# An attention and mixture-of-experts kernel: 128 tokens of the leading expert as a slot of their own, in plain fp32, and that expert first in the ring

## The chip, the cores and the metric

One core of one Trainium2 chip runs the whole kernel in one launch. The metric is device time in microseconds (us). PE is TensorE (PEld its weight loads), DVE is VectorE, ACT is ScalarE, POOL is GpSimd, SP is SyncE, from which most DMAs are issued.

## The reference

Attention with a memory term for 4 batches of 576 tokens, 8 heads of 64; its output is x (2304 tokens of 512). A gate picks one of 8 experts for each token. The expert is a two-layer network whose result is scaled by two gate factors.

```python
logits = x @ w_gate                       # 2304 x 8
e_idx = np.argmax(logits, axis=1)
probs = softmax(logits)
gate_w = probs[np.arange(N), e_idx]
eom = 1.0 / (1.0 + np.exp(-(x @ w_output_gate)))
for e in range(8):
    mask = e_idx == e
    h = np.maximum(x[mask] @ w1[e], 0.0)  # 512 -> 1024
    ye = h @ w2[e]                        # 1024 -> 512
    out[mask] = gate_w[mask, None] * eom[mask, e, None] * ye
```

On the inputs used, routing gives the eight experts 2, 465, 120, 834, 36, 680, 12 and 155 tokens. In the first two batches it gives them 0, 62, 120, 441, 2, 527, 0 and 0.

## The kernel before

**Attention.** The work is cut into jobs (scores `SS`, maxima `M`, exponentials `E`, transposes `T`, their copies `V`, values `P`, memory products `ME`, and so on), and the string `ORDER` is the order in which they are issued to the engines, written out by hand: each engine runs its own jobs in that order. Batches 0 to 2 are routed inside attention (`RT`, `RK`, `CA`, `CJ`, `CB`, `SEL`), the last one behind it. `rank` counts with small matmuls the tokens that go to an expert before each token; `cntb` carries the counts from batch to batch. The finished x goes to `xs` in DRAM, the gate factors to `gd`.

**Between attention and loop.** The last batch is routed (`route`, `rank`, `tail_rank`). From the counts come the first slot of each expert (`slots1`, `slots2`) and, through `place` (40 small matmuls into `pp`, L999) and `rows` (L1004), the token numbers of each slot. A slot is 128 tokens of one expert; tokens beyond its number are empty. `gather` (L1069) fetches a slot's x by row number; `gather_gate` (L1065) its gate factors. While PE waits, `warm` (L163) issues matmuls of ones whose results nobody reads.

**The loop.** There are 25 slots at most (NSLOT). 23 of them (NMAIN) always run; the two others stand behind a branch on the number of slots used. A product of fp32 numbers is made of three products in fp32r: x and the weights are split into a high part (a cast) and a low part (the rest), and high·high, low·high and high·low are added. `gemm1` gives h (24 matmuls of 512 columns, L1121) and its relu (ACT L1134); `stage_h` transposes h (`hp`, 8 transposes, L1144), copies it and splits it (`hh` on ACT, `hl` on POOL L1149); `gemm2` gives y (24 matmuls into `py`, L1121). `stage_x` transposes x (`px`, 4 transposes) and splits it (`xh`, `xl`). On PE the order is gemm1(s + 1), px(s + 2), the first half of gemm2(s), hp(s + 1), the second half of gemm2(s). `scatter` (L1172) writes the rows.

**Weights.** Each expert has eight raw chunks of 512 KB (four of w1, four of w2), fetched on SP's queue into a ring of five buffers. DVE casts each into `whi` (L961) and subtracts into `wlo` (L964), in turn. `whi` and `wlo` hold two experts, by the parity of the expert's turn. `sem_w` counts the chunks that are ready, and gemm waits on it. `load_expert` is the refill for turns 2 to 7: the first four chunks wait on `sem_1` until gemm1 of the last slot of the expert two turns before is done (`lim`), the last four on `sem_2` until its gemm2 is. Experts run in the order of their numbers.

```python
def load_expert(e):
    for c in range(8):
        fetch(e, c)
        if c == 0:
            lim = V.value_load(limi[0:1, e - 2:e - 1], min_val=1, max_val=NMAIN)
        if c % 4 == 0:
            V.wait_ge(sem_2 if c else sem_1, lim)
        high(e, c, V)
        low(e, c)
        ready()
```

Of the kernel before, what the change touches and what calls it, by code (L numbers as in the profile page):

```python
# [10 lines left out]
F32 = mybir.dt.float32  # L11
# [14 lines left out]
E = 8  # L26
# [8 lines left out]
NSLOT = 25  # L35
NMAIN = 23
# [46 lines left out]
N12_2 V11_3_0:ACT Tgate41 N22_2 E11_2_0 SS12_3 W2 T11_2_1 V11_2_1:ACT T11_2_0 SEL1_3 SS12_4 E12_1_0 PV2_1 T12_0 load_v14 V11_2_0:ACT E12_1_1 V12_0:ACT
M12_3_1 M12_3_0 F215 P11_256_0 G2_2 SEL1_4 M12_4_0 Y2_1 E12_3_1 E12_3_0 SS13_1 P11_256_1 M12_4_1 SEL1_2 T12_1 M13_0_0 T12_3_1 M13_1_0 O11_256:ACT
M13_0_1 V12_1:ACT M13_1_1 E12_4 XD2_1 PV2_4 PV2_3 R14 Y2_4 E13_1_1 T12_3_0 E13_0_1 SS12_2 SS13_3 XD2_4 OUT2_1 OUT2_4 V12_3_1:ACT V12_3_0:DVE M12_2_1
G2_4 E13_1_0 GA1 E13_0_0 T12_4 Y2_3 CA1 V12_4_0:ACT E12_2_1 F014 LT2_0 M12_2_0 LT2_1 T13_0 F012 SEL1_1 XD2_3 V12_4_1:DVE T13_1 LC2_0:DVE LC2_1:ACT
# [4 lines left out]
V13_4_0:ACT E14_3_1 N23_4 V13_4_1:ACT E14_1_0 SS15_4 M14_3_0 SEL0_0 T14_0 ME3_2 SS14_4 V14_0:DVE M15_4_0 N13_2 N23_2 M15_4_1 T14_1 M14_4_0 E14_3_0
M14_4_1 T14_3_0 ME3_0 SS15_1 V14_1:ACT E15_4 V14_3_0:ACT N13_0 N23_0 SS14_2 M15_0_0 T14_3_1 M15_1_1 E14_4 OUT2_0 G3_4 M15_1_0 M15_0_1 OUT2_2
V14_3_1:ACT Tgate61 fetch2 E15_0_0 P13_256_0 T14_4 CJ1 P13_256_1 P14_0_0 V14_4_0:DVE TS15_0 E15_1_1 G3_1 W3_0 CB1 V14_4_1:ACT TS15_1 O14_0:DVE
O13_256:ACT E15_0_1 TS14_1 T15_4 PLl4_0 M14_2_1 PLl1_0 V15_4_0:ACT fetch3 YLl4_0 TL4_0 E14_2_1 YLl1_0 T15_0 XLl4_0 PLl0_0 YLl0_0 V15_4_1:ACT V15_0:ACT
# [32 lines left out]
def attn_moe(ctx: ExitStack, tc: tile.TileContext, qk, vd, mz, mt, rz, beta, wgo, w1, w2, out):  # L127
# [72 lines left out]
    def rank(b):  # L200
# [7 lines left out]
        if last:  # L208
# [1102 lines left out]
```

## Time and profile before

| what | us |
|---|---|
| median of 3 runs (lowest, highest) | 515.14 (514.45, 515.40) |
| the profiled execution, its own time | 514.72 |
| its span, first to last instruction | 512.6 |
| PE busy in the span | 496.0 |
| DVE, ACT, POOL busy | 333.1, 282.0, 307.0 |
| mean granted TensorE clock | 0.994 of full |

Attention takes about the first 200 us, the loop with its start the rest. A busy PE counts every instruction in flight, dummies too. Full clock is 2.4 GHz, a granted clock of 0.50 is 1.2 GHz. An fp32 product that is not a transpose leaves two PE records, an fp32r product or a transpose one.

### The profile page before, as it was taken

How to read it: one execution, taken by the hardware profiler on the slowest of the kernel's cores; microseconds unless marked ns; L12 is line 12 of the kernel's file. 1: busy time of each engine (PE TensorE's matmuls, PEld its weight loads, DVE VectorE, ACT ScalarE, POOL GpSimd, SP SyncE). 2: the span in 40 equal slices, each digit the busy share in tenths (PEclk: the TensorE clock that was granted, in tenths of full speed). 3: DMA queues.
4: the chain of work that ended last, by engine and by line, in shares of the span. 5: the costliest groups of instructions: out<-in, count | busy, mean ns of one | idle time of the engine just before them, and what ended most of it. 6: DMA issues, size and time to landing. Idle time of an engine off the chain costs nothing.

```text
span 512.6 us, 10898 instructions
## 1 busy us (share of the span) xinstructions
PE 496.0 (97%) x3408; PEld 395.5 (77%) x3408; DVE 333.1 (65%) x819; ACT 282.0 (55%) x650; POOL 307.0 (60%) x287
## 2 busy tenths in 40 slices
PE   7999999999999998979999999999999999999995
PEld 4787778787877875557888888888888888888885
DVE  4988989889789879679898389300074892026510
ACT  5989888988787764263333344434434333333441
POOL 8756565665447327636777767565557675556333
PEclk9999999999999999989999999999999999999998
DMA  7442345241413602486687467511153674115000
GB/s 250 158 172 84 130 136 184 102 165 47 141 46 99 192 3 84 126 336 206 190 239 208 131 192 243 166 63 43 41 177 112 193 221 139 63 41 165 8 3 29
DMA packets 27233, 68.25 MB, mean 133 GB/s; under 512 B 4308, under 2 KB 4840, under 8 KB 27178
## 3 DMA queue, kind: packets, MB, share of 16 engines
q1 hardware_dynamic: 22602, 56.63, 34.6%
q0 software_dynamic: 4432, 10.77, 6.3%
q8 instruction: 33, 0.54, 0.4%
q14 instruction: 22, 0.18, 0.1%
q10 hardware_dynamic: 144, 0.13, 0.1%
HBM read 58.06 MB, written 10.76 MB: 134 GB/s over the span
## 4 chain that ended last, share of the span: by engine, by line
PE 87%; DVE 4%; DMA 3%; issue 2%; POOL 1%; ACT 1%; POOLq 0%; SPq 0%; DVEq 0%; ACTq 0%
PE h L1121 23%; PE py L1121 22%; PE po L624 9%; PE pt L589 8%; PE s L514 7%; PE me L676 4%; PE hp L1144 4%; PE sd L501 3%; PE pt L558 2%; PE px L1090 2%; DMA raw<-in_w 2%; DVE wlo L964 1%; PE pv L739 1%; PE pl L844 1%; DVE whi L961 1%
## 5 line engine op out<-in xcount | busy, mean ns | idle before, releaser
L961 DVE CAST whi<-raw 128x1024 fp32r<-128x1024 f32 x56 | 57.4, 1025 | 115.3 <-issue 82.4
L1149 POOL TENSOR_TENSOR hl<-hT,hh 128x512 fp32r<-128x512 f32 x46 | 68.3, 1505 | 73.6 <-ACT hh L1148 73.6
L964 DVE TENSOR_TENSOR wlo<-raw,whi 128x1024 fp32r<-128x1024 f32 x63 | 97.1, 1541 | 7.0 <-ACT whi L961 4.7
L1121 PE MATMUL py<-whi,hh 128*128 (+1 forms) x192 | 77.9, 406 | 0.7 <-DVEq L967 0.7
L1121 PE MATMUL h<-whi,xh 128*128 (+1 forms) x184 | 73.6, 400 | 1.8 <-ACT xh L1095 1.7
L1121 PE MATMUL h<-whi,xl 128*128 (+1 forms) x184 | 73.7, 401 | 1.6 <-POOL xl L1098 1.6
L1121 PE MATMUL py<-wlo,hh 128*128 (+1 forms) x192 | 74.2, 386 | 0.0
L1121 PE MATMUL py<-whi,hl 128*128 (+1 forms) x192 | 73.8, 384 | 0.0
L577 ACT ACTIVATE st<-st,nm 128x128 f32<-128x128 f32 (+3 forms) x128 | 71.6, 562 | 3.4 <-DVE nm L572 3.2
L1121 PE MATMUL h<-wlo,xh 128*128 (+1 forms) x184 | 73.2, 398 | 0.0
L572 DVE CUSTOM_DVE_ANT_0 st<-s,mask 128x128 f32<-128x128 f32 (+3 forms) x128 | 58.3, 483 | 9.9 <-PE s L514 5.4
L1134 ACT ACTIVATE h<-h 128x1024 f32<-128x1024 f32 x23 | 23.6, 1027 | 73.3 <-PE h L1121 73.3
L409 POOL TENSOR_TENSOR lo<-qk,hi 128x1216 fp32r<-128x1216 f32 x15 | 42.1, 2810 | 23.3 <-ACT hi L405 17.9
L1148 ACT CAST hh<-hp 128x512 fp32r<-128x512 f32 x46 | 27.6, 599 | 47.3 <-PE py L1121 47.3
L436 ACT COPY PT<-pt 128x512 f32<-128x512 f32 (+2 forms) x89 | 45.2, 523 | 15.1 <-PE pt L589 13.1
L1147 ACT COPY hT<-hp 128x512 f32<-128x512 f32 x46 | 27.2, 592 | 42.1 <-PE hp L1144 40.6
L624 PE MATMUL po<-PT,v 128*64 128x320 f32 (+4 forms) x480 | 48.9, 349 | 0.3 <-DVE gs L281 0.3
L589 PE MATMUL pt<-ident,st 128*128 128x128 f32 x320 | 47.5, 280 | 0.0
L1121 PEld LDWEIGHTS h<-whi,xh 128*128 128x128 f32 x184 | 34.9, 189 | 10.8 <-ACT xh L1095 2.2
L1121 PEld LDWEIGHTS h<-whi,xl 128*128 128x128 f32 x184 | 35.0, 190 | 10.3 <-POOL xl L1098 1.9
L624 PEld LDWEIGHTS po<-PT,v 128*64 128x64 f32 x480 | 29.7, 137 | 17.1 <-issue 2.9
L1121 PEld LDWEIGHTS py<-wlo,hh 128*128 128x128 f32 x192 | 36.1, 188 | 8.1
(204 smaller groups left out, 988.8 us busy)
## 6 DMA issues: line engine op xcount, KB each, us to landing
raw<-in_w SPq DMA_DIRECT2D x64, 512.0 KB
qk<-in_qk SPq DMA_DIRECT2D x15, 640.0 KB
v<-in_vd SPq DMA_DIRECT2D x16, 320.0 KB
xs<-xd SPq DMA_DIRECT2D x12, 256.0 KB
mz<-in_mz SPq DMA_DIRECT2D x4, 324.0 KB
mt<-in_mt SPq DMA_DIRECT2D x4, 256.0 KB
xs<-xa SPq DMA_DIRECT2D x4, 256.0 KB
xs<-xd SPq DMA_DIRECT2D x3, 128.0 KB
```

Source lines behind the costliest of these rows:

```text
L409: G.tensor_tensor(c["lo"][:, TQ:], c["raw"][:, TQ:], f32(c["hi"])[:, TQ:], op=ALU.subtract)
L436: (A.copy if e == "ACT" else V.tensor_copy)(dst(), src())
L514: T.matmul(c()["ss", q][j], l[r, lc], m[r, KC:KC + w], start=(a == 0), stop=(a == 2))
L572: V.tensor_tensor_reduce(st[:, :w], c()["ss", qt][j], mask[:, 512 - w:512], -SCALE, 3.0e38, ALU.add, ALU.min, negm()[:, i:i + 1])
L577: A.activation(st, st, AF.Exp, bias=c()["negm"][:, i:i + 1], scale=-1.0, accum_out=sums()[:, qt, 2 * p + j:2 * p + j + 1])
L589: T.transpose(pt[:, (m * k1 + i) * P:(m * k1 + i + 1) * P], st[:, i * P:(i + 1) * P], ident)
L624: T.matmul(po[64 * j:64 * j + 64, qs - q0:q1 - q0], vt[:, k, 64 * j:64 * j + 64], PT[:, j, k, qs:q1], start=(k == 0), stop=(k == kn - 1))
L961: join((A.copy if eng is A else eng.tensor_copy)(whi[:, e % 2, c, :], raws[e, c]))
L964: join(eng.tensor_tensor(wlo[:, e % 2, c, :], raws.pop((e, c)), f32(whi[:, e % 2, c, :]), op=ALU.subtract))
L1121: i = T.matmul(o[n % nh], l[:, z], m[:, n * 512 + part.start:n * 512 + part.stop], start=(c == 0 and k == 0 and n < nh), stop=(c == 3 and ...
L1148: A.copy(hh[:, z], hp[:, z])
L1149: G.tensor_tensor(hl[:, z], hT[:, z], f32(hh)[:, z], op=ALU.subtract)
```

## The change

Tokens are counted after batches 0 and 1, inside attention. The expert with the highest count there (the star) gives 128 of its tokens of these batches to a slot of its own, `e`. Its rows are found by ten small matmuls (`ZP`) and gathered; its x is transposed (`ZX`, `ZY`). The star's raw weights are fetched during attention (five chunks in place of four, at an address read from a register) and behind it (three). Its two layers are computed from the raw weights in plain fp32, 8 products of 512 columns each, spread over the stretch between attention and loop, where the `warm` matmuls are taken out.

The rest of the star's tokens come first in the ring, then the other experts in the order of their numbers: `order` holds that, and every fetch reads it. The ring has one slot less: NSLOT 24, NMAIN 22. The weights of turn 0 are split as before, but the chunks of w2 behind the star's products; turn 1 is split by DVE alone. A slot waits for all four chunks of a layer at once, except slot 0, which still waits chunk by chunk.

Smaller parts: tiles that outlive the routing stand in pools of their own; the attention outputs of odd batches stand where h32 and hT of the loop stand later; the gates of the last batch are computed behind the row numbers, beside the fp32 products; x of slot 0 is split as that of any other slot (`stage_x` in place of `first_x`).

```diff
-NSLOT = 25
-NMAIN = 23
+NSLOT = 24
+NMAIN = 22
...
 # in ORDER (new names only, with what stands around them)
+... Tpos21 CA1 CJ1 CB1 SS11_2 ... T11_4 ZC M11_2_1 E11_3_0 TS11_1 M11_2_0 Z1 Z2 Tpos31 load_v12 M12_0_0 Z3 Z4
+G2_1 V11_4_0:DVE Z5 P11_0_0 ... Tpos41 Z6 Z7 E12_0_0 Tgate21 M12_0_1 Z8 Z9 Z10 ... M12_1_1 ZN ME2_2
+... M14_3_0 SEL0_0 SEL1_0 ZK T14_0 ... T14_1 ZP M14_4_0 ZR ZG E14_3_0 ... PLl2_0 ZX YLl2_0 ZY XLl0_0 ...
+P15_512_0 fetch4 P15_0_0
...
+    def star_number():
+        V.tensor_scalar(which, ze["m"], -1.0, float(E), op0=ALU.mult, op1=ALU.add)
+        V.scalar_tensor_tensor(order[:, 1:], seven[:, 1:], which, seven[:, 1:], op0=ALU.is_ge, op1=ALU.add)
+        V.tensor_copy(order[:, 0:1], which)
...
+    def star_place():
+        ze["p"] = psm.tile([P, 1], F32, name="zp", tag="m")
+        for t in range(half_tiles):
+            T.matmul(ze["p"], selp.rearrange("p b t c -> p (b t) c")[:, t, :], stars[:, t:t + 1], start=(t == 0), stop=(t == half_tiles - 1))
...
+    def star_turn():
+        ze["px"] = pst.tile([P, 512], F32, name="pxe", tag="pt")
+        for c in range(4):
+            T.transpose(ze["px"][:, c * P:(c + 1) * P], ze["x"][:, c * P:(c + 1) * P], ident)
...
-    warm(6)
+    def star_gemm1(n, cs):
+        for c in cs:
+            T.matmul(he[:, n * 512:(n + 1) * 512], ze["x", c], raws[0, c][:, n * 512:(n + 1) * 512], start=(c == 0), stop=(c == 3))
...
+    def star_gemm2(ks):
...
+        for k in ks:
+            T.matmul(ze["py"], hTe[:, k * P:(k + 1) * P], raws[0, 4 + k // 2][:, k % 2 * 512:k % 2 * 512 + 512], start=(k == 0), stop=(k == 7))
+
+    star_gemm1(0, range(3))
     for f in route(B - 1):
         f()
     for c in range(2):
         high(0, c, A)
     rank(B - 1)
+    star_gemm1(0, range(3, 4))
+    star_relu(0)
+    star_gemm1(1, range(4))
+    star_h(0)
...
         rows(0)
         rows(1)
-        warm(10)
+        star_relu(1)
+        star_h(1)
...
-    warm(12)
     rx.close()
...
-                last = c0 + (c + 1 if s < 4 else 4)
                 if s == 0:
-                    T.wait_ge(sem_w, last + c0)
-                elif s < 4 or c == 0:
-                    T.wait_ge(sem_w, t["need", c0] + last)
+                    T.wait_ge(sem_w, c0 + c + 1)
+                elif c == 0:
+                    T.wait_ge(sem_w, t["need"] + (c0 + 4))
...
+    for c in (5, 6):
+        fetch_star(c, sx.tile([P, F], F32, name=f"star{c}", tag="raw"))
     gather(0)
+    low(0, 0)
+    ready()
+    fetch_star(7, raw_tile("star7"))
+    for f in fin["gates"][0]:
+        f()
+    for c in range(2, 4):
+        high(0, c, A)
+    gather_gate("e")
     gather(1)
...
+    for c in range(1, 4):
         low(0, c)
         ready()
...
+    star_gemm2(range(6))
+    stage_x(0)
+    for f in fin["gates"][1]:
+        f()
+    star_gemm2(range(6, 8))
+    finish_star()
     counts()
+    gather_gate(0)
+    gather(2)
+    gemm1(0, lambda: stage_x(1))
+    regs(1)
+    gather_gate(1)
+    gather_gate(2)
+    gather(3)
+    for c in range(4, 8):
+        split(0, c, V)
+    for c in range(8):
         fetch(1, c)
+        split(1, c, V)
```

## Rows read from the trace of the kernel before

**Rows 1.** The page, part 4: the chain that ended last, by engine
```profile
PE 87%; DVE 4%; DMA 3%; issue 2%; POOL 1%; ACT 1%; POOLq 0%; SPq 0%; DVEq 0%; ACTq 0%
```

**Rows 2.** Windows: stretch, PE, PEld, DVE, ACT, POOL busy (instructions), clock, DMA, GB/s
```profile
100.00:200.00 100.00, 99.32 (x1001) 78.80 (x998) 85.59 (x342) 75.72 (x213) 50.34 (x59) 1.00 0.31 102
```

**Rows 3.** Timeline, 190 to 225: start, us, engine, line, operation, out<-in, count [idle <-releaser]
```profile
198.27 1.35 PE L844 MATMUL pl<-rzt,oT 128*128 128x160 f32 x8
...
199.77 1.46 PE L163 MATMUL warm<-ones 128*128 128x512 bf16 x6
...
202.86 1.89 PE L163 MATMUL warm<-ones 128*128 128x512 bf16 x8
...
205.38 1.16 PE L999 MATMUL pp<-hit,selp 128*128 128x4 f16 x40 [0.64 <-DVE hit L996]
206.06 0.16 DVE L1004 TENSOR_SCALAR rowi<-pp 128x4 int32<-128x4 f32 x1 [0.32 <-PE pp L999]
...
212.93 0.50 PE L1121 MATMUL h<-whi,xh 128*128 128x512 f32 x1
...
220.41 0.58 ACT L1095 CAST xh<-px 128x512 fp32r<-128x512 f32 x1
...
221.56 1.47 POOL L1098 TENSOR_TENSOR xl<-x,xh 128x512 fp32r<-128x512 f32 x1 [3.39 <-ACT x L1097]
```

**Rows 4.** Chain in order of time, 200 to 300: start, us, engine, tile, line, count
```profile
207.94 3.79 DMA xr<-xs,rowi
...
215.89 7.88 DMA raw<-in_w
...
238.93 5.60 PE h L1121 x24
```

**Rows 5.** Chain in order of time, 340 to 420
```profile
357.15 0.44 PE px L1090 x4
357.59 2.81 PE py L1121 x12
360.39 0.87 PE hp L1144 x8
361.27 2.80 PE py L1121 x12
364.06 5.60 PE h L1121 x24
...
401.60 5.60 PE h L1121 x24
```

**Rows 6.** Timeline of DVE, 262 to 513: the refill of the weights
```profile
370.92 0.71 DVE L961 CAST whi<-raw 128x1024 fp32r<-128x1024 f32 x1 [45.30 <-issue]
...
391.47 1.53 DVE L961 CAST whi<-raw 128x1024 fp32r<-128x1024 f32 x1 [9.60 <-ACTq L1128]
...
402.67 1.60 DVE L961 CAST whi<-raw 128x1024 fp32r<-128x1024 f32 x1 [0.87 <-issue]
404.30 2.20 DVE L964 TENSOR_TENSOR wlo<-raw,whi 128x1024 fp32r<-128x1024 f32 x1
406.64 0.69 DVE L961 CAST whi<-raw 128x1024 fp32r<-128x1024 f32 x1
407.37 1.23 DVE L964 TENSOR_TENSOR wlo<-raw,whi 128x1024 fp32r<-128x1024 f32 x1
...
411.55 2.51 DVE L964 TENSOR_TENSOR wlo<-raw,whi 128x1024 fp32r<-128x1024 f32 x1
```

**Rows 7.** Timeline of POOL, 398 to 416
```profile
402.43 3.00 POOL L1149 TENSOR_TENSOR hl<-hT,hh 128x512 fp32r<-128x512 f32 x2 [3.81 <-ACT hh L1148]
...
411.67 1.30 POOL L1098 TENSOR_TENSOR xl<-x,xh 128x512 fp32r<-128x512 f32 x1
```

**Rows 8.** Windows of PE alone: stretch, PE busy (instructions), clock, DMA, GB/s
```profile
223.00:223.50 0.50, 0.41 (x1) 0.50 1.01 362
...
226.00:226.50 0.50, 0.50 (x4) 0.75 1.03 385
```

More of the change, by code (lines that the diff above doesn't have):

```diff
@@ L83 @@
[L83 to L86, printed above, removed]
@@ L91 @@
[L91 to L94, printed above, removed]
@@ L99 @@
-OL4 RX2 GO1 RK2 V15_2_0:ACT CA2 Tpos12 Tgate32 Tpos22 Tgate22 CJ2 T15_2_1 Tpos32 Tgate42 V15_2_1:ACT GA2 CB2 Tgate52 P15_384_0 O15_384:ACT P15_256_0
-Tpos42 Tgate62 TL0_1 TL3_0 XLl3_0 XLl0_1 PLl3_1 G3_3 SEL2_0 OL1 O15_256:ACT SEL2_3 SEL2_2 SEL2_4 G3_2 SEL2_1 PLl2_1 YLl3_1 YLl2_1 XLl3_1 XLl2_1 GP2
-GS2 OL0 OL2 OL3 GO2 TL2_1 TL3_1
+V10_4_0:ACT MW3 T11_0 M11_4_0 Tpos11 M11_3_0 load14 TS10_1 V10_4_1:ACT V11_0:ACT MC3 T11_1 M11_3_1 V11_1:ACT ME2_4 Tpos21 CA1 CJ1 CB1 SS11_2 M11_4_1
+E11_4 SS12_1 E11_3_1 N12_4 N22_4 T11_4 ZC M11_2_1 E11_3_0 TS11_1 M11_2_0 Z1 Z2 Tpos31 load_v12 M12_0_0 Z3 Z4 G2_1 V11_4_0:DVE Z5 P11_0_0 TS11_0
@@ L154, in attn_moe @@
     less = const.tile([P, E], BF16, name="less")
-    back = const.tile([P, E], F32, name="back")
+    back = const.tile([P, NEND], F32, name="back")
+    star = const.tile([P, E], F32, name="star")
+    rest8 = const.tile([P, E], F32, name="rest8")
+    order = const.tile([P, E], I32, name="order")
+    seven = const.tile([P, E], F32, name="seven")
+    later = const.tile([P, E], F32, name="later")
+    gone = const.tile([P, NEND], F32, name="gone")
+    which = const.tile([P, 1], F32, name="which")
+    stars = const.tile([P, NQ * 2], F16, name="stars")
+    begin = const.tile([P, E], F32, name="begin")
+    rowe = const.tile([P, 1], I32, name="rowe")
+    lg3 = const.tile([P, NQ, 16], F32, name="lg3")
+    gs3 = const.tile([P, P], F32, name="gs3")
+    dl3 = const.tile([P, NQ, E], F32, name="dl3")
+    og3 = [const.tile([P, NQ], F32, name=f"{n}3") for n in ("og", "gw")]
+    ze = {}
     ohe = const.tile([P, B * NQ, E + 1], F32, name="ohe")
@@ L925, in attn_moe, with star_total @@
         pair(g)
-    for c in range(4):
-        job(f"fetch{c}", "SP", 400, 60 + 2 * c, fetch, 0, c, after=[f"load{NG - 1}", "R15"] + ([f"fetch{c - 1}"] if c else []), takes=[("qa" if c < 2 else "hi", f"raw{c}")], size=512)
+    for c in range(5):
+        job(f"fetch{c}", "SP", 400, 60 + 2 * c, lambda c: fetch_star(c) and None, c)
+    half_tiles = 2 * NQ
+    jc = ohe[:, :half_tiles, E]
+    def star_total():
+        ze["n"] = psm.tile([P, E], F32, name="zn", tag="m")
+        T.matmul(ze["n"], ones, cntb, start=True, stop=True)
@@ L928, in attn_moe, with star_columns_of @@
+    def star_columns_of():
+        for c in range(4):
+            A.copy(ze["x", c], ze["px"][:, c * P:(c + 1) * P])
+    job("ZY", "ACT", 800, 0.0, star_columns_of)
     for b in range(B):
@@ L1180, in split @@
         ready()
+    for c in (5, 6):
+        fetch_star(c, sx.tile([P, F], F32, name=f"star{c}", tag="raw"))
     gather(0)
+    low(0, 0)
[6 more added lines that the diff above has]
+    gather_gate("e")
     gather(1)
-    gather(2)
-    for c in range(2):
+    for c in range(1, 4):
         low(0, c)
         ready()
-    low(0, 3, G)
-    for c in range(2):
-        fetch(1, c, sx, None if c else st[0]["x"][0:1, 0:1])
-    low(0, 2)
-    ready()
-    first_x()
-    for s in range(3):
-        gather_gate(s)
-    V.tensor_copy(top[0:1, 0:1], f32(wlo)[0:1, 0, 3, 0:1])
-    ready()
-    counts()
-    for c in (2, 3):
-        fetch(1, c)
-    for c in range(2):
-        split(1, c, A)
-    def second():
-        stage_x(1)
-        for c in (2, 3):
-            split(1, c, A)
-    gemm1(0, second)
-    regs(1)
-    gather(3)
-    for e in range(2):
-        for c in range(4, 8):
-            fetch(e, c)
-            split(e, c, V)
+    star_gemm2(range(6))
[4 more added lines that the diff above has]
+    finish_star()
+    counts()
+    gather_gate(0)
[8 more added lines that the diff above has]
+    for c in range(8):
+        fetch(1, c)
+        split(1, c, V)
     for s in range(NMAIN):
```

241 lines of the change are left out of this document (163 added, 78 removed).

## The prediction, made before the changed kernel ran

> **What bounds the kernel now.** I read the chain of waits by engine first [rows 1]: 87% of the span is TensorE (PE), so a change counts where it alters PE's queue or makes PE wait. Then the windows: in attention PE is busy 99.32 of 100 us, with VectorE (DVE) at 85.59 beside it [rows 2], so matmuls added there lengthen it one for one, while DVE work has some slack.
>
> Then the stretch between attention and loop [rows 3]. PE is never off for long there, but much of what it does is dummy work: the 8 `warm` matmuls after the rank take 1.89 us, and 36 are issued in all, at 0.24 us some 8.5 us. They hold nothing up: the slot positions (`pp`, 40 small matmuls) come at 205.38, when DVE delivers `hit`, and the row numbers at 206.06. The chain of that stretch [rows 4] shows the gather of the first tokens (3.79 us), and later 7.88 us of waiting for raw weights. Slot 0's first product is at 212.93 and slot 2's at 238.93. What PE computes between is 2 first products, 1 second product and their transposes.
>
> Last, the loop [rows 5]. One period is px 0.44, 12 py 2.81, hp 0.87, 12 py 2.80, 24 h 5.60: 12.52 us, without gap. A slot fewer is worth **12.52 us** if nothing else stalls. By these lengths the work from slot 0's first product to slot 2's is 5.60 + 0.44 + 5.60 + 0.87 + 0.44 + 2.81 + 0.87 + 2.80 = 19.43 us; it took 26.00. So the start loses 6.6 us, since slots 0 and 1 belong to two experts whose weights are still arriving.
>
> **What the new order of experts does.** The reference's routing on its inputs gives 2, 465, 120, 834, 36, 680, 12 and 155 tokens: slots 1, 4, 1, 7, 1, 6, 1, 2, in all 23. Expert 5 leads the first half with 527. With 128 of its tokens taken out and itself in front, the ring is 5 (slots 0 to 4), 0 (slot 5), 1 (6 to 9), 2 (10), 3 (11 to 17), 4 (18), 6 (19), 7 (20, 21): 22 slots, exactly NMAIN. Slots 0 to 4 now share weights, which takes away the waits at the start. But at the end two experts of one slot each, 4 and 6, stand together, and there were never two before: 1 and 4, 1 and 7, 1 and 6 alternate.
>
> Weights live in two buffers by parity of turn; DVE refills them strictly in turn (`load_expert`): the first half of an expert waits until gemm1 of the last slot that uses the buffer is done, the second half for its gemm2. In the trace of before the turn after the 7 slots of expert 3 shows what this costs [rows 6]. gemm1 of slot 12, the last of them, ends at 369.66 [rows 5]; DVE, idle for 45.30 us, starts at 370.92; the second half waits for gemm2 until 391.47; the next expert's first half starts only at 402.67 and its last low part ends at 414.06 (411.55 + 2.51). In the old order that expert was not needed for several slots. In the new order the same pattern follows slot 17: turn 6 (expert 6) takes the place of the load at 370.92, and turn 7 (expert 7) that of the load at 402.67, and gemm1 of slot 20 needs the latter. Laid over the old trace, gemm1 of the third slot after the last starts at 401.60 [rows 5], and with it must wait until about 413. Queued behind that wait on PE are gemm2 of slot 19, whose weights are ready, and everything after.
>
> **The sum, part by part.**
> (a) One slot removed: -12.52.
> (b) That stall. While PE stands, GpSimd (POOL) soon has nothing to do. A cast and a subtraction beside POOL's hl took 1.60 and 2.20; without it 0.69 and 1.23 [rows 6, 7]. The 2.51 at 411.55 lies beside the POOL subtraction at 411.67, which would not be there; with 1.23 the load ends at 412.78, with 0.15 for drain and semaphore PE starts at 412.93: 412.93 - 401.60 = **+11.3**. Bounds: four free chunks, 4 x 2.09 = 8.4 from 402.67, give +9.6; the load as slow as in the trace +12.6. I take 11.3, the row changed only where its cause is gone.
> The Trainium skill (GPSIMD Engine Reference, Key points) says that GpSimd shares its SBUF interfaces with VectorE and contends with instructions in a two-port mode or with two SBUF inputs. By it alone, with POOL called idle from the start of the stall, the term would be the +9.6, and the total 1.7 us lower.
> (c) The clock after the stall. Slot 1 had to wait for its tokens; when its matmuls resumed at about 223 the granted clock was 0.50, the 1.2 GHz level, and it came back between 226 and 226.5 [rows 8]. Some 3.2 us ran at half speed: +1.5 lost, and once more here. An idle of 11 us should cost no less than one of 4; bounds +0.8 to +2.5.
> (d) Attention. PE gets `ZC` and `ZP`, 11 small matmuls at 1.16/40 = 0.03, and four transposes 0.44 [rows 3, 5]: +0.75, all on the path at 99% busy. DVE gets 15 small operations at 0.16 (like `rowi`): 2.4 us in short bursts, against some 14% slack; I take +0.4 on PE, bounds 0 and 2.4. ACT's 4 copies, POOL's constants, one gather, SEL1_0 and SP's fifth fetch lie beside other work. The moved CA1, CJ1 and CB1 only change places; their input is old by then. Sum **+1.15** (0.75 to 3.2).
> (e) The stretch between. Price of a plain fp32 product of 512 columns, which the trace lacks: four products of 160 columns leave 8 records in 1.35 us [rows 3], 0.34 each with the tail, times 3.2 is 1.08 at most; four passes like the one-pass products of the loop (5.60/24 = 0.233) are 0.93. The records overlap their tails, so I take 0.90; 16 products cost 14.4, up to 17.3 at the bound.
> The Trainium skill (FP8 and Floating Point Precision) counts four passes for true fp32; at 2.4 GHz that is an estimate of 0.85 per product, and the start would come 0.7 us earlier by it.
> In order: three products run from 199.8 to 202.5 in place of `warm(6)`, while DVE routes the last batch; the rank (done at 202.86 before) is not held up. Five more products, 4.5, now stand ahead of `pp` where 8 dummies stood: 207.4; four transposes: 207.8; `pp` 1.16 ends at 209.0 instead of 206.54, so the row numbers come 2.6 us later. The gather, formerly issued at 207.94, goes at 208.9 and lands at 212.7. PE meanwhile does four transposes and six products (5.4) until 215.15, px 0.44, the transposed gates, the last two products (1.8) until 217.5. Chunks 5 to 7 of the weights must land in that time; they have 3 us or more. Slot 0's xl now comes by two ACT copies and POOL instead of pieces on DVE: from first copy to its end 223.03 - 220.41 = 2.6 in the trace [rows 3], so 218.4. Full pace from 218.2, 5.3 later than 212.93. From there 19.43, plus 0.6 to 0.8 because POOL issues a scatter and two gathers ahead of xl of slot 1: slot 2 at 238.4 against 238.93. **-0.5**; bounds -1.5 (all waits hidden) and +4 (1.08 per product, late chunks, or DVE late with the second-layer weights, which it has ready only some 1 to 2 us ahead by my count).
> Each slot now sets one wait per product on full halves; all of those weights are old except at slot 20. Sum: -12.52 + 11.3 + 1.5 + 1.15 - 0.5 = **+0.9**.
>
> The sum stands against the profiled execution: span 512.6, its time 514.72, so 2.1 lie outside and stay; that execution is 0.4 below the median 515.14. 514.72 + 0.9 = 515.6, 515.14 + 0.9 = 516.0; I forecast **515.8**, no change that can be told: 0.2%, 1.0 us, is about what this measurement separates.
>
> **Rivals.**
> 1. The stall isn't there or hides: then (b) and (c) fall out, 515.8 - 12.8 = 503.0. It needs turn 7's first half ready within 32 us of slot 17's gemm1. Against it: DVE's order and the rows at 391.47 and 402.67. 0.10.
> 2. Slower: the fp32 block becomes the bound between attention and loop. Place: PE's queue from 202.86 on, where all later work waits behind 13 products and what feeds them. At 1.08 a product it is 2.3 us longer; late chunks or DVE's late second-layer weights add 1 to 2 more: 518 to 521. It decides from 0.95 us a product or a first full-pace product after 219.5. For it: the bound of the price; against it: four passes of 0.233. 0.18.
> 3. The start gains what it can: the -1.5 of (e), (b) at 9.6, (c) at 0.8: 511.9 to 513.5. 0.10.
> 4. My forecast, 513.5 to 518: 0.62. Of it 0.10 lies below 514.1 and 0.22 above 516.2.
> That the change doesn't do what it says: expert 5 leads by 527 to 441, and 22 slots fit NMAIN, so the branch for leftover slots isn't entered.
>
> **Chances.** Faster 0.10 + 0.10 + 0.10 = 0.30, same 0.30, slower 0.18 + 0.22 = 0.40. The range 512 to 520 leaves out rival 1 and the edges of 2 and 3.
>
> **What would show it.** (a) 22 slots of 12.52. (b) One idle stretch of PE of 10 to 12 us just ahead of the third slot from the end, ended by DVE's wlo. (c) Granted clock 0.50 behind it. (d) Attention longer by about 1 us. (e) fp32 products of two records near 0.45 each; slot 2 near 239.5. If PE has no gap near slot 20, (b) is wrong and the time near 503; if slot 2's first product is at 242 or later, rival 2 holds.

## The result, and the profile after

| | us | against before |
|---|---|---|
| before, median of 4 (lowest, highest) | 514.80 (514.35, 515.40) | |
| after, median of 4 (lowest, highest) | 520.08 (519.82, 521.25) | 1.0106 [1.0086, 1.0126] |
| after, the profiled execution | 521.25, span 519.5 | |

The change makes the kernel slower by 1.1%, some 5.3 us; the forecast was 515.8, with a range from 512 to 520. Of the length of the profiled execution 1.05 us are no part of the change: between 8.6 and 12 us its granted clock is halved, before any work of the change, and in the profiled execution of before it isn't. The same loss stands in seven of the fourteen traces used here, `a2_before_swap56` among them, which holds nothing of the change; `a3_half_early`, which holds all of it, is among the seven without. So the traces are compared by distances between two marks, not by absolute times, and medians that lie 1 us apart may do so by this alone.

The chain of waits by engine, the row of after that answers to [rows 1]. PE's share falls, the shares of DVE and POOL rise, though neither works much more than before:

```profile
PE 85%; DVE 5%; POOL 4%; issue 2%; DMA 1%; ACT 1%; ACTq 0%; DVEq 0%; POOLq 0%
```

The marks, first of before, then of after: four groups of memory products of attention (`me`), the last transposition of the gates (`gp`) with which attention ends for PE, and the transposition of slot 3's tokens (`px`), which stands right behind gemm1 of slot 2. Timeline of PE: start, us, engine, line, operation, tiles, shape, count.

```profile
120.38 1.02 PE L676 MATMUL me<-mz,phi 64*128 64x81 f32 x16
...
134.73 1.12 PE L676 MATMUL me<-mz,phi 64*128 64x81 f32 x16
...
142.21 1.12 PE L676 MATMUL me<-mz,phi 64*128 64x81 f32 x16
...
164.87 1.07 PE L676 MATMUL me<-mz,phi 64*128 64x81 f32 x16
...
199.66 0.28 PE L277 MATMUL gp<-ident,og 128*5 128x128 f32 x1
...
244.37 0.60 PE L1090 MATMUL px<-ident,xr 128*128 128x128 f32 x4
```

```profile
121.42 1.02 PE L717 MATMUL me<-mz,phi 64*128 64x81 f32 x16
...
135.77 1.12 PE L717 MATMUL me<-mz,phi 64*128 64x81 f32 x16
...
144.10 1.12 PE L717 MATMUL me<-mz,phi 64*128 64x81 f32 x16
...
166.76 1.07 PE L717 MATMUL me<-mz,phi 64*128 64x81 f32 x16
...
203.18 0.27 PE L294 MATMUL gp<-ident,og 128*5 128x128 f32 x1
...
250.35 0.60 PE L1243 MATMUL px<-ident,xr 128*128 128x128 f32 x4
```

From the first `me` to `gp` it is 79.28 us before and 81.76 after: attention is **2.48** longer. From `gp` to `px` 44.71 and 47.17: the stretch between attention and loop, with slots 0 to 2, is **2.46** longer. From `px` to the end of the span 268.23 and 269.15: the rest is **0.92** longer, though it has one slot fewer. The difference of 1.04 at the first `me` is the start's, and in the middle 0.85 is lost between 135.77 and 144.10 alone (8.33 against 7.48).

The stretch between, after, which answers to [rows 3]. Timeline of PE:

```profile
203.29 2.74 PE L1100 MATMUL he<-star 128*128 128x512 f32 x6
...
208.18 3.70 PE L1100 MATMUL he<-star 128*128 128x512 f32 x8 [0.69 <-ACT h32e L1104]
...
212.16 1.16 PE L1152 MATMUL pp<-hit,selp 128*128 128x4 f16 x40
...
214.05 5.32 PE L1118 MATMUL pye<-star,hTe 128*128 128x512 f32 x12
...
222.36 0.50 PE L1272 MATMUL h<-whi,xl 128*128 128x512 f32 x1 [0.50 <-POOL xl L1251]
...
238.41 0.50 PE L1272 MATMUL py<-whi,hl 128*128 128x512 f32 x1 [2.42 <-POOL hl L1300]
```

A product of fp32 is two records; 8 records in 3.70 us are 0.93 a product, and 12 in 5.32 are 0.89. PE has three waits above 0.3 us: 0.69 for ACT's relu, 0.50 for slot 0's xl, and 2.42 at 238.41 for `hl` of slot 0. The last is answered by POOL's timeline:

```profile
227.13 1.64 POOL L1251 TENSOR_TENSOR xl<-x,xh 128x512 fp32r<-128x512 f32 x1
228.92 1.88 POOL L1225 DMA_INDIRECT g<-gd,rowi  x1 [0.15 <-DMA out<-ye,rowe]
231.10 1.79 POOL L1225 DMA_INDIRECT g<-gd,rowi  x1 [0.30 <-issue]
233.19 1.79 POOL L1234 DMA_INDIRECT xr<-xs,rowi  x1 [0.30 <-issue]
235.29 1.78 POOL L1225 DMA_INDIRECT g<-gd,rowi  x1 [0.30 <-issue]
237.09 2.51 POOL L1300 TENSOR_TENSOR hl<-hT,hh 128x512 fp32r<-128x512 f32 x2
```

Behind xl of slot 1 come two gate gathers, the gather of slot 3's tokens and its gate gather, from 228.92 to 237.07, and only then `hl`, whose first inputs ACT had ready at 233.64 (its cast of `hh` starts at 233.05 and takes 0.59).

The stall near the end: first the timeline of PE, then DVE's, then windows of 1 us (columns as in [rows 2]), last the chain in order of time.

```profile
481.56 0.79 PE L1272 MATMUL h<-whi,xh 128*128 x1 [11.29 <-DVEq L1091]
```

```profile
471.35 1.54 DVE L1085 CAST whi<-raw 128x1024 fp32r<-128x1024 f32 x1 [0.86 <-issue]
472.93 2.17 DVE L1088 TENSOR_TENSOR wlo<-raw,whi 128x1024 fp32r<-128x1024 f32 x1
475.23 0.69 DVE L1085 CAST whi<-raw 128x1024 fp32r<-128x1024 f32 x1
475.96 1.22 DVE L1088 TENSOR_TENSOR wlo<-raw,whi 128x1024 fp32r<-128x1024 f32 x1
```

```profile
473.00:474.00 1.00, 0.00 (x0) 0.00 (x0) 1.00 (x1) 0.00 (x0) 1.00 (x1) 0.50 0.82 309
482.00:483.00 1.00, 1.00 (x4) 0.71 (x4) 0.97 (x2) 0.00 (x0) 0.00 (x0) 0.50 0.58 221
485.00:486.00 1.00, 1.00 (x4) 0.71 (x4) 0.86 (x2) 0.00 (x0) 0.00 (x0) 0.50 0.09 16
487.00:488.00 1.00, 1.00 (x6) 0.81 (x5) 0.86 (x2) 0.00 (x0) 0.00 (x0) 1.00 0.00 0
```

```profile
481.56 8.08 PE h L1272 x24
```

PE stands still for 11.29 us ahead of gemm1 of slot 20, released by DVE's semaphore (slot 20 is the last but one of the ring's 22; the prediction and two of the expectations below call it the third from the end); DVE is at the first half of the last expert. The granted clock is 0.50, the 1.2 GHz level, from the window at 473 on, PE having stood since 470.27, and 1.00 again at 487. The 24 products take 8.08 us in place of 5.60: 2.48 lost.

So -12.52 + 11.29 + 2.48 for the rest, +2.48 for attention, +2.46 for the stretch between: +6.2. The spans differ by 6.9 with the 1.05 of the start, 5.85 without; the 0.3 between lie in the rest (1.25 by its terms, 0.92 by the marks) and were not followed.

### The profile page after: what moved, and what is told of

Its sections match the earlier page's. It is cut to its first block, busy times and chain, and to the rows that moved or that the text cites. A ratio compares the mean times of both kernels' runs of the same rounds, so it can differ in the third digit from the quotient of the medians.

```text
span 519.5 us, 10832 instructions
## 1 busy us (share of the span) xinstructions
PE 494.7 (95%) x3367; PEld 391.5 (75%) x3367; DVE 339.3 (65%) x843; ACT 276.5 (53%) x645; POOL 306.1 (59%) x288
## 4 chain that ended last, share of the span: by engine, by line
PE 85%; DVE 5%; POOL 4%; issue 2%; DMA 1%; ACT 1%; ACTq 0%; DVEq 0%; POOLq 0%
PE h L1272 21%; PE py L1272 21%; PE po L661 9%; PE pt L626 8%; PE s L551 7%; PE me L717 4%; PE hp L1295 3%; PE sd L538 3%; DVE wlo L1088 2%; PE pt L595 2%; PE px L1243 2%; DVE whi L1085 1%; PE he L1100 1%; PE pye L1118 1%; PE pv L780 1%
## 5 line engine op out<-in xcount | busy, mean ns | idle before, releaser
L1085 DVE CAST whi<-raw 128x1024 fp32r<-128x1024 f32 x56 | 51.2, 914 | 111.1 <-ACTq L1279 82.4
L1300 POOL TENSOR_TENSOR hl<-hT,hh 128x512 fp32r<-128x512 f32 x44 | 63.4, 1465 | 64.3 <-ACT hh L1299 64.2
L1088 DVE TENSOR_TENSOR wlo<-raw,whi 128x1024 fp32r<-128x1024 f32 x56 | 91.5, 1634 | 1.9
L1272 PE MATMUL h<-whi,xh 128*128 (+1 forms) x176 | 71.2, 405 | 11.3 <-DVEq L1091 11.3
L1272 PE MATMUL py<-whi,hh 128*128 (+1 forms) x184 | 74.3, 404 | 0.0
L1272 PE MATMUL py<-whi,hl 128*128 (+1 forms) x184 | 70.9, 385 | 2.4 <-POOL hl L1300 2.4
L1272 PE MATMUL h<-whi,xl 128*128 (+1 forms) x176 | 70.8, 402 | 0.7 <-POOL xl L1251 0.7
L1272 PE MATMUL py<-wlo,hh 128*128 (+1 forms) x184 | 70.8, 385 | 0.0
L1272 PE MATMUL h<-wlo,xh 128*128 (+1 forms) x176 | 70.4, 400 | 0.0
L1251 POOL TENSOR_TENSOR xl<-x,xh 128x512 fp32r<-128x512 f32 x22 | 29.6, 1347 | 24.6 <-ACT x L1250 18.8
L1272 PEld LDWEIGHTS py<-whi,hl 128*128 128x128 f32 x184 | 34.7, 189 | 8.5 <-POOL hl L1300 2.7
```

The costliest lines, as they stand in the source:

```text
L1085: join((A.copy if eng is A else eng.tensor_copy)(whi[:, e % 2, c, :], raws[e, c]))
L1088: join(eng.tensor_tensor(wlo[:, e % 2, c, :], raws.pop((e, c)), f32(whi[:, e % 2, c, :]), op=ALU.subtract))
L1251: G.tensor_tensor(xl, x32, f32(xh), op=ALU.subtract)
L1272: i = T.matmul(o[n % nh], l[:, z], m[:, n * 512 + part.start:n * 512 + part.stop], start=(c == 0 and k == 0 and n < nh), stop=(c == 3 and ...
L1300: G.tensor_tensor(hl[:, z], hT[:, z], f32(hh)[:, z], op=ALU.subtract)
```

## The experiments

Times of before were taken with each group of runs; ratios are against those. The theory after the traces: **T1**, the stall comes from two adjacent experts of one slot behind DVE's fixed order, and it is the stall that halves the clock; **T2**, the stretch between loses its 2.5 us to POOL's queue; **T3**, attention loses to the place of the new DVE and ACT work. Against T1 stands that DVE's rate is too low for one slot fewer, against T2 that the fp32 block itself is the bound (the second rival of the prediction), against T3 that the work costs the same anywhere.

### Another order of the experts, after and before

Experts 6 and 7 exchanged in after, and experts 5 and 6 in before, as a permutation of the arrays (the edit of after stands here; in before `turn` is [0, 1, 2, 3, 4, 6, 5, 7]):

```diff
-    wgo = np.concatenate([inputs['moe_w_gate'], inputs['moe_w_output_gate']], axis=1).reshape(NP, 2, D, 16)
+    turn = [0, 1, 2, 3, 4, 5, 7, 6]
+    wgo = np.concatenate([inputs['moe_w_gate'][:, turn], inputs['moe_w_output_gate'][:, turn]], axis=1).reshape(NP, 2, D, 16)
...
-        beta=inputs['beta'], wgo=wgo, w1=inputs['moe_w1'], w2=inputs['moe_w2'],
+        beta=inputs['beta'], wgo=wgo, w1=inputs['moe_w1'][turn], w2=inputs['moe_w2'][turn],
```

> The kernel after with experts 6 and 7 exchanged in the arrays (gate columns and both weight arrays), so that the ring is 5, 1, 4, 1, 7, 1, 2, 1 slots: no two single slots stand next to each other behind a full ring. Theory 'adjacent single slots': the 11.3 us idle stretch of PE ahead of the third slot from the end is gone and with it the 2.2 us that the halved clock behind it costs: 520.1 - 13.5 = 506.6 us (506 to 507.5). Rival 'DVE can't keep pace once one slot less stands ahead': the late half comes late in another order too, an idle stretch of about 10 us stands elsewhere, 516 us or more.

Measured 507.69 us, 0.9846 [0.9818, 0.9874], 0.2 us above the range expected. Its trace has the loss at the start, and PE's wait for `hl` of slot 0 (2.40 us) nearly as after; behind that no idle stretch of PE is left in the loop.

> The kernel before with experts 5 and 6 exchanged in the arrays, so that its ring is 1, 4, 1, 7, 1, 1, 6, 2 slots: two single slots adjacent, and nothing of the change in it. Theory 'adjacent single slots': the same stall as after, 11.3 us, and some 2 us at half clock behind it: 514.8 + 13.5 = 528.3 us (526.5 to 529.5), PE idle ahead of the first slot of the seven-turn ring's sixth change. Rival 'the stall belongs to the new slot 0 or to fetching by register': 514.8 us as before.

Measured 529.34 us, 1.0265 [1.0228, 1.0301], as expected. The kernel before, with nothing of the change in it, has the same stall. Timeline of PE:

```profile
413.96 0.79 PE L1121 MATMUL h<-whi,xh 128*128 x1 [11.29 <-DVEq L967]
```

Its length is that of after to the hundredth, 11.29. The first part of T1 holds: two adjacent experts of one slot make the stall with or without the change, so neither the fetch by register nor the extra slot is its cause, and since it goes in another order of the experts, DVE's rate alone isn't either.

### The last expert's first half ahead of the last but one's second

```diff
-        if s < E - 2:
-            load_expert(s + 2)
+        if s < E - 4:
+            load_expert(s + 2)
+        elif s == E - 4:
+            load_expert(E - 2, range(4))
+            load_expert(E - 1, range(4))
+        elif s == E - 3:
+            load_expert(E - 2, range(4, 8))
+            load_expert(E - 1, range(4, 8))
```

PE's waits count accordingly (not shown here): gemm1 of turn 7 waits for 56 chunks in place of 60, gemm2 of turn 6 for 60 in place of 56.

> The kernel after, with the first half (w1) of the last expert loaded ahead of the second half (w2) of the last but one, data as they are: the order of DVE's work is w1(6), w1(7), w2(6), w2(7) by turns, and PE's waits count accordingly. Theory 'DVE's order, not its rate': w1 of the last turn is ready some 7 us before the product that needs it, w2 of the last but one some 2 us before, so no idle stretch and no halved clock: 506.6 us (506 to 508). Rival 'DVE's rate': the wait moves to w2 of the last but one, 512 us or more.

Measured 504.90 us, 0.9799 [0.9770, 0.9827]. Groups of PE's products in the last fifth (busy us, mean ns | idle ahead of them), then DVE at the starts and ends of its halves, last the two products that need them, from the chain in order of time:

```profile
L1282 PE MATMUL h<-whi,xh 128*128 x56 | 22.3, 399 | 0.0
```

```profile
449.32 0.71 DVE L1085 CAST whi<-raw 128x1024 fp32r<-128x1024 f32 x1 [1.16 <-ACTq L1289]
...
458.49 2.20 DVE L1088 TENSOR_TENSOR wlo<-raw,whi 128x1024 fp32r<-128x1024 f32 x1
460.89 0.69 DVE L1085 CAST whi<-raw 128x1024 fp32r<-128x1024 f32 x1 [0.20 <-issue]
...
470.19 2.20 DVE L1088 TENSOR_TENSOR wlo<-raw,whi 128x1024 fp32r<-128x1024 f32 x1
```

```profile
467.49 5.60 PE h L1282 x24
...
473.53 2.80 PE py L1282 x12
```

No idle time stands ahead of these products, nor ahead of the others of the last fifth. DVE now works from 449.32 on with no wait longer than 0.20 us; the first half of turn 7 is ready at 460.7, 6.8 us before the product that needs it (467.49), the second half of turn 6 at 472.4, 1.1 us before its own (473.53). The same work, in another order, hides. This kernel came 1.7 us below the 506.6 expected, under its range: its wait for `hl` of slot 0 is 0.84 us in place of 2.42, since three of POOL's gathers ahead of it took 1.0 to 1.2 us, which took 1.65 to 1.9 after. With that its `gp` to `px` is 45.17.

### PE kept busy through the stall

```diff
                 elif c == 0:
+                    if s == 20 and c0 == 0:
+                        w = pm.tile([P, 512], F32, name="keep", tag="px")
+                        for _ in range(48):
+                            T.matmul(w.rearrange("p (a c) -> p a c", c=P), ones, ones.unsqueeze(1).to_broadcast([P, 4, P]), start=True, stop=True)
                     T.wait_ge(sem_w, t["need"] + (c0 + 4))
```

> The kernel after, with 48 bf16 products of 128x512 on a constant tile put into PE's queue just ahead of the wait of the third slot from the end, some 10.2 us at 0.213 us each; nothing reads what they make. Theory 'the half clock behind the stall comes from PE having stood still': the stall keeps its end, the clock stays at 1.00 behind it, and 2.2 us are saved: 517.9 us (517.4 to 518.4). Rival 'the drop has another cause, or the stall's end moves with PE's activity': 520.1 us or more.

Measured 519.17 us, 1.0076 [1.0050, 1.0102]. Timeline of PE, then a window of that trace:

```profile
469.90 10.53 PE L1270 MATMUL keep<-ones 128*128 128x512 bf16 x48
481.36 0.49 PE L1276 MATMUL h<-whi,xh 128*128 x1 [0.93 <-DVEq L1091]
```

```profile
482.00:484.00 2.00, 2.00 (x10) 1.61 (x9) 1.83 (x3) 0.00 (x0) 0.00 (x0) 1.00 0.36 137
```

The stall ends where it ended, the clock stays at 1.00, and the products behind run at full pace (24 in 5.86 us by the chain, 8.08 after). From the first of them to the end of the span it is 35.54 us against 37.94: 2.4 saved in the trace. The medians differ by 0.9 only, and by the ratios 1.5; the profiled execution has the halved clock at its start too, as after, and the interval is 2.7 us wide. So it is shown that the clock behind the stall is halved when PE has stood still and isn't when it has worked; the price of 2.4 to 2.5 us stands by the trace alone.

### POOL's queue

```diff
-        if s > 2:
+        if s > 3:
             gather_gate(s)
...
     gemm1(0, lambda: stage_x(1))
     regs(1)
-    gather_gate(1)
-    gather_gate(2)
-    gather(3)
...
             regs(s + 2)
+        if s == 0:
+            gather(3)
+            gather_gate(1)
+            gather_gate(2)
+        if s == 1:
+            gather_gate(3)
```

> The kernel after with POOL's queue reordered: the gate gathers of slots 1 and 2 and the gather of slot 3 no longer stand between xl of slot 1 and hl of slot 0, but behind xl of slot 2; slot 3's gate behind xl of slot 3. Nothing else is moved. Theory 'POOL's queue behind the start of the loop': hl of slot 0 starts as soon as ScalarE's copies are there, near 233.7 instead of 237.1 us, PE's 2.42 us wait for it goes, slot 2's first product comes near 242.5 instead of 244.9, and the time is 520.1 - 2.4 = 517.7 us (517.2 to 518.5). Rival 'POOL is behind anyway': the four gathers hold up xl or hl of the next slots, the wait shows up one slot later, 519.5 us or more.

Measured 516.96 us, 1.0036 [1.0022, 1.0050], a little below what was expected. POOL's timeline and the chain:

```profile
232.74 3.15 POOL L1300 TENSOR_TENSOR hl<-hT,hh 128x512 fp32r<-128x512 f32 x2 [4.96 <-ACT hh L1299]
```

```profile
241.25 5.61 PE h L1272 x24
```

`hl` starts 30.53 us behind `gp` in place of 33.91, PE's wait is gone, gemm1 of slot 2 runs next to its neighbours without a gap, and `gp` (202.21) to `px` (246.70) is 44.49, against 47.17 after and 44.71 before. T2 holds: reordering the queue alone gives back 2.68 us in the trace, more than the 2.46 that the stretch had lost, and no wait came one slot later.

### The fp32 block

Two small edits: the halves of the first product in two PSUM tiles, and slot 0's tokens transposed two products earlier.

```diff
-    he = pa.tile([P, F], F32, name="he", tag="h", bufs=2)
+    he = [pa.tile([P, F], F32, name=f"he{n}", tag="h", bufs=2) for n in range(2)]
...
-    star_gemm2(range(6))
+    star_gemm2(range(4))
     stage_x(0)
...
-    star_gemm2(range(6, 8))
+    star_gemm2(range(4, 8))
```

> The kernel after with two small changes between attention and loop: the two halves of the fp32 slot's first product go to two PSUM tiles instead of one, so that the second half doesn't wait until ScalarE has read the first (0.69 us), and slot 0's tokens are transposed after four of the eight second products instead of six, so that POOL's xl of slot 0 is ready before PE comes to it (0.50 us). Theory 'PE's own work sets the start of the loop': both waits go, slot 0's second product comes near 221.2 instead of 222.4 us, 518.9 us (518.6 to 519.3). Rival 'the gathers set it': 222.4 and 520.1 us as now.

Measured 518.02 us, 1.0046 [1.0032, 1.0060]. Timeline of PE:

```profile
204.96 4.54 PE L1100 MATMUL he<-star 128*128 128x512 f32 x10
...
234.34 0.50 PE L1272 MATMUL py<-whi,hl 128*128 128x512 f32 x1 [1.07 <-POOL hl L1300]
```

The ten records run through without the 0.69 us wait. Up to `px` of slot 2 the stretch is 1.31 shorter (30.68 us from `gp`, 31.99 after), as expected. The wait for `hl` shrinks by 1.35 too, and that was not expected: POOL begins the extra slot's scatter 0.95 us earlier behind `gp`, and three operations of its queue ahead of `hl` (xl of slot 1 and the two gate gathers behind it) take 1.7 us less in sum than after. The time lies below the 518.6 to 519.3 written down.

Then the price of the block itself. 13 of its 16 products are left out (each of the three kept ones starts and ends its sum), so the rows of the extra slot hold other numbers:

```diff
-        for c in cs:
+        for c in [c for c in cs if c == 0]:
...
-        for k in ks:
+        for k in [k for k in ks if k == 0]:
```

> The kernel after with 13 of the extra slot's 16 fp32 products left out (of each half of the first product, and of the second product, only the first 128 rows of the sum are kept), so the rows of the extra slot are not the reference's; all else, its transposes, copies, loads, gather and scatter, stays. 13 products at 0.92 us are 11.9 us of PE. Theory 'the block fills time in which PE would wait': the ranking, the gathers and the split weights set the start of the loop then, and only 2 to 4.5 us come back, 515.6 to 518.1 us. Rival 'the block stands on the path': all of it comes back, 508 to 509 us.

Measured 521.76 us, 1.0100 [1.0068, 1.0131]: nothing comes back, and neither theory had that. Timeline of PE and windows of its trace:

```profile
204.73 0.19 PE L221 MATMUL rk<-oha,upper 128*128 128x40 bf16 x1 [1.73 <-DVE oha L256]
...
215.74 1.09 PE L1243 MATMUL px<-ident,xr 128*128 128x128 f32 x4 [2.09 <-DVE wlo L1088]
```

```profile
206.00:210.00 4.00, 3.34 (x28) 2.14 (x29) 2.58 (x13) 0.93 (x3) 0.97 (x1) 0.50 0.40 137
...
218.00:222.00 4.00, 2.79 (x7) 1.97 (x7) 3.75 (x18) 0.70 (x2) 3.46 (x3) 0.50 0.31 67
```

PE now waits 1.73 for the routing and 2.09 for DVE's low parts, its clock is at 0.50 from 206 to 222, and `gp` (201.86) to `px` (247.28) is 45.42: of 11.9 us left out, 1.75 come back in this trace. Most of the time that the block takes is time that PE would spend waiting or computing at half clock. What the block costs beside a PE kept at full clock isn't known: a run with dummies in the place of the 13 products, as before had them there, wasn't made. The profiled execution took 517.77 us; of the five, two lie near 517.8 and three near 521.9, and what the three others lose is open. That all 11.9 us come back, the expectation's rival, falls in either case.

### The new work in attention

The extra slot's transposes and ACT's copies of them 4 us later:

```diff
-... PLl2_0 ZX YLl2_0 ZY XLl0_0 ... O14_256:ACT YLl1_1 ...
+... PLl2_0 YLl2_0 XLl0_0 ... O14_256:ACT ZX ZY YLl1_1 ...
```

> The kernel after with the four transposes of the extra slot's tokens and ScalarE's four copies out of PSUM (ZX and ZY in the order) moved some 4 us later, behind the evacuation O14_256 where ScalarE has a gap of 2.3 us. Theory 'place': PE's 0.41 us wait at 191.7 and half of the delay of that stretch go, the last transposition of the gates comes at 202.6 instead of 203.2: 519.5 us (519.2 to 519.8). Rival 'amount': the 0.67 us of transposes cost the same wherever they stand beside a PE that is never idle: 520.1 us.

Measured 520.46 us, 1.0102 [1.0086, 1.0118]: no change that the time can tell. In the trace `me` (120.14) to `gp` (201.32) is 81.18 against 81.76, the 0.58 expected. The transposes and the copies were moved together, so the 0.58 isn't divided between PE and ACT.

DVE's counting of batch 1 and its choice of the expert at other places, in two forms (the first added line is `b3_choice_late`, the second is part of `c2_best`, further down):

```diff
-... Tpos21 CA1 CJ1 CB1 SS11_2 ... ZC M11_2_1 ... Z1 Z2 Tpos31 ... Z3 Z4 G2_1 ...
+... Y2_3 CA1 CJ1 CB1 V12_4_0:ACT E12_2_1 ZC F014 LT2_0 M12_2_0 Z1 Z2 LT2_1 ...
+... Y2_3 CA1 CJ1 CB1 V12_4_0:ACT ... LY2 ZC P12_0_0 ... SEL0_4 load_v13 Z1 Z2 ...
```

> The kernel after with VectorE's counting of batch 1 (CA1, CJ1, CB1) at the place that it has in the kernel before, and the choice of the leading expert (ZC, Z1 to Z10, ZN) spread behind it by pairs over the next dozen entries. Theory 'place': the 0.85 us that attention lost between 124 and 142 came from a burst of small VectorE work in the chain, and spread out it hides: 519.3 us (519.0 to 519.7). Rival 'amount': VectorE is busy 90% there as well, the same 2.5 us of work costs as much at any place: 520.1 us (519.8 to 520.6).

Measured 524.31 us, 1.0173 [1.0156, 1.0189], above what either theory had. Timeline of PE:

```profile
157.17 0.17 PE L974 MATMUL zn<-cntb,ones 128*128 128x8 bf16 x1 [2.18 <-DVE nm L609]
...
161.43 1.09 PE L626 MATMUL pt<-ident,st 128*128 128x128 f32 x4 [2.35 <-DVE PT L473]
```

The 0.85 between 135.75 and 143.24 is gone, but PE comes to `ZC`, a product of 0.17 us, 2.18 us before DVE has its input, and all later work of PE in attention is queued behind it; 2.35 us of waiting for DVE follow. Attention is 87.90 long, 6.1 more than after.

### The parts together

> The kernel after with the last expert's first half loaded early, hl of slot 0 ahead of the gathers on POOL, the two PSUM tiles, and slot 0's tokens transposed after four of the second products. If the parts add up: 504.9 (early half alone) - 2.7 (POOL's queue) - 1.3 (PE's two waits, the part of the gain that doesn't come through the shorter wait for hl): 500.9 us (500.2 to 501.7). If the start of the loop has another limit behind them (the split weights of expert 1 on VectorE, the next gathers): 502 us or more.

Measured 503.39 us, 0.9762 [0.9741, 0.9784]. `gp` to `px` is 42.98, 2.19 less than in `a3_half_early`, where 4.0 were expected, and the time lies above the 500.2 to 501.7 written down: the two gains overlap, since that kernel waited for `hl` only 0.84 us (0.84 and the 1.31 of PE's two waits make 2.15).

> c1_best_start with the transposes of the extra slot's tokens 4 us later in attention, and VectorE's counting of batch 1 at its place of before, with PE's count product (ZC) put some 4 us behind it so that PE doesn't wait for it, and the choice behind that. Theory 'place': the 0.58 us that the later transposes gave and the 0.86 us of the burst between 135 and 142 both go: 1.4 us less than c1_best_start, 499.5 us (499 to 500.3). Rival 'VectorE's work costs as much at the other place': 0.6 less or nothing.

Measured 504.76 us, 0.9801 [0.9780, 0.9822]: 1.4 more, not 1.4 less. With `ZC` later PE doesn't wait for it, but DVE's backlog holds PE elsewhere. Timeline of PE:

```profile
156.20 0.63 PE L626 MATMUL pt<-ident,st 128*128 128x128 f32 x4 [0.84 <-DVE PT L473]
...
163.82 1.30 PE L661 MATMUL po<-PT,v 128*64 128x320 f32 x8 [1.53 <-DVE y L784]
166.11 1.85 PE L661 MATMUL po<-PT,v 128*64 128x256 f32 x20 [1.00 <-DVE y L784]
```

Attention is 84.45 long, 3.3 more than with the late transposes alone. At two other places the burst cost more than at its own. So of T3 this much is left: the place of the transposes and copies costs 0.58 us, by the traces alone; the place of DVE's burst matters too, against the rival "costs the same anywhere", but no place was found at which it is cheaper.

> c1_best_start with the transposes of the extra slot's tokens and their copies some 4 us later in attention, as in b2_turn_late, and VectorE's choice of the expert left where the change put it. If the gain seen in that trace (attention 0.58 us shorter) adds to the rest: 503.4 - 0.6 = 502.8 us (502.0 to 503.5), attention 81.2 us from the memory products near 121 to the last transposition of the gates instead of 81.75. If not: 503.4 us or more.

Measured 501.93 us, 0.9740 [0.9722, 0.9759], the lowest of all: 2.6% below before, and attention 81.18 as in `b2_turn_late`, 0.56 less than in `c1_best_start`. The medians of the two differ by more than that, but their intervals overlap, so the traces show this gain and the times don't. From the page of its profile, part 4:

```profile
PE 93%; DVE 2%; issue 1%; POOL 1%; DMA 1%; ACT 0%; SPq 0%; POOLq 0%; ACTq 0%; DVEq 0%
```

## Why the prediction missed, step by step

The time fell just outside the range, on its slow side. Of the sum, (a) and (b), the two large terms, came as forecast. What failed is, in order of size, (e), whose count of POOL's queue stopped too early (2.96 us off), (d), which took two pieces of work as covered (1.33), and (c), which took the price of a shorter idle stretch (0.98).

| term | forecast | measured in the trace |
|---|---|---|
| (a) a slot less | -12.52 | -12.52 |
| (b) the stall | +11.3 (9.6 to 12.6) | +11.29 |
| (c) the clock behind it | +1.5 (0.8 to 2.5) | +2.48 |
| (d) attention | +1.15 (0.75 to 3.2) | +2.48 |
| (e) the stretch between | -0.5 (-1.5 to +4) | +2.46 |
| sum | +0.9 | +6.2; spans without the start's 1.05: +5.85 |

**(a) and (b) were right.** 22 slots of 12.51 us, and a stall foreseen to within 0.05 us (412.93 - 401.60 = 11.33, measured 11.29), by laying the new ring over DVE's old rows [rows 5, 6] and changing only the row whose cause was gone. The first pair of the late half took 1.54 and 2.17 us beside POOL's hl, the next 0.69 and 1.22 without it. The Trainium skill (GPSIMD Engine Reference, Key points) names the shared SBUF interfaces as a cause of such contention. The trace agrees in these two pairs; the +9.6 worked out with POOL idle from the start of the stall didn't come, since POOL worked until 476.05.

**(c) was mis-sized.** I took the loss behind slot 1's wait [rows 8], some 3.2 us at half clock, as the price. Here PE computed at half clock from 481.56 to past 486. That an idle stretch of 11 us costs no less than one of 4 was written; the value taken was that of the shorter one all the same. The 2.48 lies within the bounds, at their upper end.

**(d) was mis-sized** at two covers. ACT's four copies were put down as beside other work; PE waits 0.41 us for ACT ahead of a `po` of 28 records behind them, and 0.58 us goes when they and the transposes move. DVE's burst was taken at 0.4 with "some 14% slack" [rows 2]; at its place it cost 0.85 (that much goes in `b3_choice_late`, where the burst is taken away from there). That "CA1, CJ1 and CB1 only change places" overlooked that DVE's slack over 100 us says nothing about the 6 us in which the burst runs. The rest, 1.05, is near the 0.75 put down for PE; no run tried it.

**(e) failed** at one sentence: "plus 0.6 to 0.8 because POOL issues a scatter and two gathers ahead of xl of slot 1". The count stopped at xl of slot 1. Behind it the change puts the gate gathers of slots 1 and 2, which before were done by 218.2, ahead of `hl` of slot 0; with slot 3's two gathers that is 8.2 us of POOL's queue, and in `b1_hl_first`, with them behind `hl`, the stretch is -0.22 against before, where -0.5 was forecast. What stood ahead of that sentence held nearly: the gather of the first tokens was issued 1.4 us later than forecast (213.87, or 210.35 in before's time, against 208.9), but PE had products to do meanwhile. A product cost 0.89 to 0.93, forecast 0.90. The Trainium skill (FP8 and Floating Point Precision, TensorE Precision Notes) gives four passes for true fp32, from which the prediction had its estimate of 0.85; the measured value is the one to use. Slot 0's second product came at 222.36, which is 218.84 in before's time (less 3.52, by which `gp` came later), forecast 218.4.

**The rivals.** The second gave 518 to 521, and the time fell into it, by another mechanism. Its two conditions were not met: a product stayed under 0.95 us, and the first product at full pace came before 219.5 in before's time. But the sign that was to decide for it, slot 2's first product at 242 or later, was: that sign counts with slot 2 near 239.5, the forecast's own delay of attention included, and slot 2 came at 244.91, past 242 even without the start's 1.05. The sign was badly chosen, as it tells that slot 2 is late and not what made it late. `b1_hl_first` tells that: with the block as it is and POOL's queue reordered, the lateness of the stretch goes. The first rival (no stall, 503.0) is what the kernel would be with the order of DVE changed: 504.9. With the stall gone the change is worth 10 us, with POOL's queue and the two small waits mended as well 12 (`c1_best_start`), and with the extra slot's transposes later too 13 (`c3_best_late_turn`); as it stands, the stall, the clock behind it and the 4.9 us of (d) and (e) take all of it back and more.

## What to carry to other kernels

When an edit reorders the units that share a ring of buffers, lay the new sequence over the old rows of the refilling engine and look for two short units in a row: that stall was foreseen to within 0.05 us, and loading the last unit's first half ahead of the second half of the one before hid it. When an edit moves work on a queue, go on counting that queue up to the next thing that the bounding engine needs, not only to the first. And a busy share over a long stretch is no cover for a burst: price it by the rows where it lands.

## What the runs showed that was not expected

- Taking 11.9 us of products from PE saved no time in the median and 1.75 us in the trace: PE's granted clock fell to 0.50 while it waited, and the rest ran at that level, 1.2 GHz, from 206 to 222.
- One and the same indirect DMA took POOL 0.94 to 1.3 us to issue in some places and 1.65 to 1.9 in others. Before and after, every long one ran beside DVE's casts or subtractions of a chunk, but some beside them were short, so what decides is open; the wait for `hl` was 2.42, 1.07 or 0.84 us in kernels whose queues on POOL are the same.
- DVE's subtraction of a chunk (1.23 us alone) took 4.94 us when it ran beside POOL's hl and xl (at 236.98 after).
- A product of 0.17 us placed ahead of its input on PE, with DVE's backlog of that stretch, made attention 6 us longer, as everything behind it waited.
